# Products of the identity in TensorE's first idle time, and a scheduler that serves GpSimd before VectorE

## The chip, the cores and the metric

The kernel runs on one core of a Trainium2 chip, as one program and one launch. The metric is the device time of that launch in microseconds (us); smaller is better. The core has five engines with queues of their own: TensorE (PE; its weight loads are listed as PEld), VectorE (DVE), ScalarE (ACT), GpSimd (POOL) and SyncE (SP), which here only issues DMAs. Each engine takes its instructions strictly in the order of its own queue and waits at an instruction until what that one needs is there.

## The reference, cut to what matters

Three stages, all in float32. `x` is (8, 8, 512, 64): batch, heads, tokens, width; `state` is (8, 8, 32, 64).

```python
scores = scale * np.matmul(x, state.transpose(0, 1, 3, 2))     # softmax over the 32 states
xread  = np.matmul(softmax(scores), state)
scores2 = scale * np.matmul(state, x.transpose(0, 1, 3, 2))    # softmax over the 512 tokens
sread  = np.matmul(softmax(scores2), x)
x = concatenate([xread, sread], axis=2)     # to rows: 4608 x 512
x = (x @ w_a) * (x @ w_b) @ w_out           # first gated layer, 512 -> 1536 -> 512
g = x @ w_gate
out = silu(g) * (x @ w_val) @ w_out2        # second gated layer
```

The weights come as float64 words; the kernel makes float32 values of them on the chip. Products are made from two-part splits, three products for each (high by high, high by low, low by high).

## The kernel before

**Work and stages.** Tokens are worked on in blocks 0 to 7 of 512 columns and a block "s" with the 256 state rows. For the first layer the kernel multiplies states and weights first (`state_w`, tiles `sw`): each result goes to DRAM and comes back as `swr`, is split by ScalarE and VectorE into `swh` and `swl`, and TensorE then needs only the 32-wide softmax weights (`xs`) against it (`p`, line L624), followed by the output product `po` (L659). A name such as `p_1_2_0` is block 1, slice 2 of the inner 1536, side a. Blocks 0 to 3 take their first four slices in turn (list `TOGETHER`), so the early program is: scores `psc` (L505), softmax, `sw` products, `p` of blocks 0 and 1, and so on. The second layer (L729, L823) fills the second half of the program.

**Early chains.** A weight tile (`raw_w`, `raw_wo`) is loaded, converted by two ScalarE passes, a clamp (L384), a shift (L389) and a sign pass (L392) on VectorE and an integer add on GpSimd (L396). Then it is split: a ScalarE cast (L422 or L345) and a VectorE subtract (L338). `w_1` below is the second set of such tiles; `swl_0` is the low half that block 0 or 1 needs for slices 0 and 1, `swl_1` the one for slices 2 and 3.

**What sets the order.** `Program.order` is a list scheduler that runs while the program is built. Each piece of work is a Task with a planned duration for every engine that could do it, and a due time `by`. Time is advanced event by event; for each free engine the ready task with the earliest due time is taken, and the order of these picks becomes the order of the engines' queues. VectorE work with SBUF operands alone (`port`) and all GpSimd work exclude each other in the plan (`shared`, `blocked`). Engines are served in the order of the dict `ready`:

```python
ready = {e: [] for e in ("PE", "ACT", "DVE", "POOL", "DMA")}
```

Some subtracts, multiplies and clamps may go to VectorE or GpSimd (`dve_pool`). Short TensorE tasks are planned at double time as long as the main products have not begun (`main <= self.first`). The chip follows the queues alone; the planned times do not exist there.

Of the kernel before, what the change touches and what calls it, by code (L numbers as in the profile page):

```python
# [10 lines left out]
F32 = mybir.dt.float32  # L11
# [7 lines left out]
P = 128  # L19
# [41 lines left out]

ACT_US, DVE_US, FAST_US, POOL_US = ((0.09, 0.84e-3), (0.07, 1.05e-3), (0.07, 0.53e-3), (0.2, 2.6e-3))
# [3 lines left out]

BESIDE_US = 0.9
# [8 lines left out]
def dve(n, fast=False):  # L76
    a, b = FAST_US if fast else DVE_US
    return {"DVE": a + b * n}


def dve_pool(n):
    return dve(n) | {"POOL": POOL_US[0] + POOL_US[1] * n}
# [13 lines left out]
class Task:  # L96
    def __init__(self, i, engines, fn, bufs, deps, by, start, size):
        self.i, self.engines, self.fn, self.bufs, self.deps = i, engines, fn, bufs, deps
        self.by, self.start, self.size = by, start, size
        self.cost = min(engines.values())  # L100
        self.next = []
        self.new = []
        self.engine, self.main = None, 0.0

        self.port = False


class Program:
# [37 lines left out]
    def order(self):  # L146
# [4 lines left out]
        for t in reversed(tasks):  # L151
            for n in t.next:
                t.by = min(t.by, n.by - n.cost - HOP_US - (DMA_US + n.size / DMA_BYTES_PER_US if n.size else 0))
# [6 lines left out]
        main = 0.0  # L160
        ready = {e: [] for e in ("PE", "ACT", "DVE", "POOL", "DMA")}
# [12 lines left out]
        now, done = 0.0, []  # L174
        while events:
            now = events[0][0]
            main = max(main, min(now, self.first))
            while gates and gates[-1].start <= main:
                t = gates.pop()
# [4 lines left out]
            while events and events[0][0] <= now + 1e-9:  # L184
                _, kind, _, t = heapq.heappop(events)
# [8 lines left out]
            for e, heap in ready.items():  # L194
                if free[e] > now + 1e-9:
                    continue
                held = []
                blocked = shared > now + 1e-9 and e in ("DVE", "POOL")
                while heap:
                    item = heapq.heappop(heap)  # L200
                    t = item[2]
# [10 lines left out]
                    if e == "POOL" and "DVE" in t.engines and sum(  # L212
                        q[2].engines["DVE"] for q in ready["DVE"] if q[2].engine is None and not q[2].port
                    ) < BESIDE_US:
                        held.append(item)
                        continue
# [11 lines left out]
                    us = t.engines[e] * (2.0 if e == "PE" and t.engines[e] < 1.0 and main <= self.first else 1.0)  # L228
# [31 lines left out]
class Kernel:  # L260
# [80 lines left out]
    def hi_lo(self, src_buf, src, hi_buf, hi, lo_buf, lo, n, psum=False, **kw):  # L341

        hb = (hi_buf, 0) if hi_buf is lo_buf else hi_buf
        lb = (lo_buf, 1) if hi_buf is lo_buf else lo_buf
        self.p.add(act(n), lambda e: self.nc.scalar.copy(hi(), src()), [src_buf], [hb], **kw)  # L345
        self.subtract(
            lo, src, lambda: hi().bitcast(F32), dve(n) if psum else dve_pool(n), [src_buf, hb], [lb], **kw
        )
# [17 lines left out]
    def convert(self, src, name, start=0.0, by=1e9):  # L366

        nc = self.nc
# [13 lines left out]
        def clamp(e):  # L382
            f = t.t[:, 0].bitcast(F32)
            self.by_engine[e].tensor_scalar(  # L384
                out=f, in0=f, scalar1=SATURATED, scalar2=-SATURATED, op0=ALU.min, op1=ALU.max
            )

        self.p.add(dve(512, True) | {"POOL": 1.9}, clamp, [], [hi], **kw)
# [124 lines left out]
    def softmax1(self, b, g, sT, by):  # L513
# [11 lines left out]
        self.p.add(dve_pool(512), lambda e: self.by_engine[e].tensor_tensor(  # L525
# [14 lines left out]
        self.p.add(dve_pool(512), lambda e: self.by_engine[e].tensor_tensor(  # L540
# [6 lines left out]
    def softmax2(self, b, g, sT, by):  # L547
# [38 lines left out]
        self.pe(1.75, fn, [a2, xn], [ps], **kw)  # L586
# [277 lines left out]
    def body(self):  # L864
# [3 lines left out]
        p.add({"POOL": 1.2}, lambda e: make_identity(nc, self.ident.t), [], [self.ident], by=0.0)  # L868
        self.sread = Buf(None, "sread", lambda: self.sb.tile([P, NPAIR, ST], F32, name="sread"))
# [159 lines left out]
```

## Time and profile before

| | us |
|---|---|
| median of 3 runs (1513.57 to 1515.39) | 1514.61 |
| the profiled execution, its own time | 1514.56 |
| span of its trace | 1512.8 |
| TensorE busy in the span | 1471.7 (97%) |
| VectorE busy | 1069.6 (71%) |
| ScalarE busy | 649.5 (43%) |
| GpSimd busy | 111.9 (7%), 84 instructions |

The span runs from the first to the last instruction of the trace. Busy shares are means over stages that differ, so the rows further down are taken from stretches. In rows of the timeline the first two numbers are the start and the length in us, "x4" counts merged instructions, and the square bracket gives the idle time in front and what ended it. A float32 product that is not split shows as two MATMUL records.

### The profile page before, as it was taken

The numbers are of one execution on the slowest core, as the hardware profiler recorded it, in microseconds if no ns is written. First come the engines' busy times: TensorE is split into PE (matmuls) and PEld (weight loads), VectorE is DVE, ScalarE is ACT, GpSimd is POOL, SyncE is SP. The second block draws the span as 40 slices with busy tenths as digits, with TensorE's granted clock in tenths as the row PEclk, the third lists the DMA queues.
The fourth block names the chain that finished last, engine by engine and source line by source line (L and its number), as shares of the span: only waits on it lengthen the run. The fifth ranks groups of instructions, "written<-read, shape, count | busy, mean of one in ns | idle before, by whom it ended". The sixth has DMA issues, their size and how long they took to land.

```text
span 1512.8 us, 19096 instructions
## 1 busy us (share of the span) xinstructions
PE 1471.7 (97%) x6760; PEld 1213.7 (80%) x6760; DVE 1069.6 (71%) x1792; ACT 649.5 (43%) x1148; POOL 111.9 (7%) x84
## 2 busy tenths in 40 slices
PE   5699999999999999999999999999999999999998
PEld 2477788788888888998888888888888888888887
DVE  7989848865778787776777996556854677535554
ACT  6567756653556565654433441222322223222220
POOL 2212201200011111111000100000000000000000
PEclk7899999999999999999999999999999999999999
DMA  8575554652556565765965796455573456423412
GB/s 305 182 277 181 200 213 179 212 207 97 179 190 216 181 232 207 251 233 203 386 246 204 280 354 233 170 183 208 220 259 128 161 192 221 182 99 138 155 56 70
DMA packets 111183, 305.87 MB, mean 202 GB/s; under 512 B 11760, under 2 KB 12784, under 8 KB 111088
## 3 DMA queue, kind: packets, MB, share of 16 engines
q1 hardware_dynamic: 111088, 304.66, 56.1%
q8 instruction: 53, 0.87, 0.2%
q14 instruction: 42, 0.34, 0.1%
HBM read 223.35 MB, written 80.74 MB: 201 GB/s over the span
## 4 chain that ended last, share of the span: by engine, by line
PE 80%; DVE 1%; DMA 0%; issue 0%; ACT 0%; SPq 0%; DVEq 0%; ACTq 0%
PE pu L823 17%; PE po L659 12%; PE p L624 11%; PE pC L729 9%; PE pB L729 9%; PE pA L729 9%; PE pD L729 4%; PE p_s L624 2%; PE pvs L624 1%; PE po_s L659 1%; PE pgs L624 1%; PE pus L823 1%; PE psr L584 1%; PE psc L505 1%; DMA swr<-sw 0%; PE sw L452 0%
## 5 line engine op out<-in xcount | busy, mean ns | idle before, releaser
L659 PE MATMUL po<-hs,wo 128*128 128x512 f32 x1152 | 285.5, 392 | 0.0
L659 PEld LDWEIGHTS po<-hs,wo 128*128 128x128 f32 x1152 | 215.6, 188 | 45.2 <-issue 1.0
L624 PE MATMUL p<-xs,swh 128*128 128x512 f32 x768 | 240.2, 394 | 1.0 <-DVE xs L338 0.5
L624 PEld LDWEIGHTS p<-xs,swh 128*128 128x128 f32 x768 | 144.0, 189 | 32.0 <-DVE a L643 1.1
L624 PE MATMUL p<-xs,swl 128*128 128x512 f32 x384 | 150.7, 392 | 9.0 <-DVE swl L338 8.8
L729 PE MATMUL pB<-x,w 128*128 128x512 f32 x576 | 146.2, 389 | 0.0
L729 PE MATMUL pA<-x,wg 128*128 128x512 f32 x576 | 146.2, 389 | 0.0
L823 PE MATMUL pu<-wo,hv 128*128 128x512 f32 x576 | 140.6, 390 | 0.0
L823 PE MATMUL pu<-wo,hu 128*128 128x512 f32 x576 | 138.5, 390 | 0.0
L729 PEld LDWEIGHTS pB<-x,w 128*128 128x128 f32 x576 | 108.2, 188 | 22.4
L729 PEld LDWEIGHTS pA<-x,wg 128*128 128x128 f32 x576 | 108.2, 188 | 22.4
L823 PEld LDWEIGHTS pu<-wo,hu 128*128 128x128 f32 x576 | 107.9, 188 | 22.2
L823 PEld LDWEIGHTS pu<-wo,hv 128*128 128x128 f32 x576 | 107.9, 188 | 22.2
L743 DVE TENSOR_TENSOR t<-c,pB 128x512 f32<-128x512 f32 x96 | 65.9, 686 | 82.5 <-PE pB L729 81.4
L643 DVE TENSOR_TENSOR a<-a,p 128x512 f32<-128x512 f32 x96 | 65.8, 685 | 79.5 <-PE p L624 68.4
L747 ACT ACTIVATE av<-t 128x512 f32<-128x512 f32 x48 | 30.3, 632 | 175.9 <-DVE t L743 175.8
L330 ACT COPY a<-p 128x512 f32<-128x512 f32 x81 | 47.5, 586 | 105.4 <-PE p L624 100.0
L624 PEld LDWEIGHTS p<-xs,swl 128*128 128x128 f32 x384 | 72.6, 189 | 25.1 <-DVE swl L338 9.8
L345 ACT CAST hs<-a 128x512 fp32r<-128x512 f32 x96 | 59.6, 621 | 60.5 <-DVE a L643 52.5
L338 DVE TENSOR_TENSOR hs<-a,hs 128x512 fp32r<-128x512 f32 x96 | 69.5, 725 | 14.0 <-ACT hs L345 13.3
L841 DVE TENSOR_TENSOR part<-part,pu 128x512 f32<-128x512 f32 x64 | 43.9, 685 | 47.5 <-PE pu L823 47.3
L729 PE MATMUL pC<-x,wv 128*128 128x512 f32 x288 | 73.2, 390 | 0.0
(175 smaller groups left out, 2343.1 us busy)
## 6 DMA issues: line engine op xcount, KB each, us to landing
w<-w SPq DMA_DIRECT2D x120, 512.0 KB, 5.1
sw<-swo SPq DMA_DIRECT2D x96, 256.0 KB, 2.5
wg<-w2g SPq DMA_DIRECT2D x48, 512.0 KB, 4.7
wv<-w2v SPq DMA_DIRECT2D x48, 512.0 KB, 4.9
wo<-w2o SPq DMA_DIRECT2D x48, 512.0 KB, 5.6
swr<-sw SPq DMA_DIRECT2D x47, 512.0 KB, 4.9
raw_w<-in_wab SPq DMA_DIRECT2D x24, 512.0 KB, 7.7
xt<-in_xt SPq DMA_DIRECT2D x32, 256.0 KB, 5.3
```

The costliest lines, as they stand in the source:

```text
L330: self.nc.scalar.copy(out(), in_())
L338: lambda e: self.by_engine[e].tensor_tensor(out=out(), in0=in0(), in1=in1(), op=ALU.subtract), r, w, **kw
L345: self.p.add(act(n), lambda e: self.nc.scalar.copy(hi(), src()), [src_buf], [hb], **kw)
L505: pe.matmul(ps.t, lhsT=l, rhs=r, start=n == 0, stop=n == len(pairs) - 1)
L624: pe.matmul(ps.t[:, :n], lhsT=l, rhs=r, start=i == 0, stop=i == last)
L643: self.vec(n, lambda v, a=a, pb=pb: v.tensor_tensor(out=a.t[:, :n], in0=a.t[:, :n], in1=pb.t[:, :n], op=ALU.mult), [pb], [a])
L659: pe.matmul(ps.t[:, :n], lhsT=wo[f].t[:, hw, c], rhs=hs.t[:, hh, :n], start=st, stop=sp)
L729: pe.matmul(ps.t, lhsT=w.t[:, hw, c], rhs=x.t[:, hx], start=start and i == n == 0, stop=stop and i == 1 and n == 2, skip_group_check=True)
L743: self.vec(512, lambda e: e.tensor_tensor(out=out.t, in0=ta(), in1=tb(), op=op), [a, b], [out])
L747: p.add(act(n), lambda e: nc.scalar.activation(out=a.t[:, :n], in_=g.t[:, :n], func=AF.Sigmoid), [g], [a])
L823: pe.matmul(ps.t, lhsT=h.t[:, hh, c], rhs=wo[f].t[:, hw], start=f == steps[0] and i == 0, stop=f == steps[-1] and i == 2)
L841: self.vec(w, lambda v: v.tensor_tensor(out=to(), in0=part.t[:, j % 2, :w], in1=ps.t[:, :w], op=ALU.add), [ps, (part, j)], [ok], by=by)
```

## The change: what it does

It adds 44 tasks, each of two 128x128 products of the identity with itself into a PSUM tile `warm` that nothing reads. Their due time is the latest of all and they take no part in the due times of others (`spare`); TensorE gets one wherever the plan finds it free. The scheduler serves GpSimd ahead of VectorE. Tasks that VectorE or GpSimd could do now belong to VectorE alone, and the rule with `BESIDE_US` is gone. Short TensorE tasks are planned at double time only in the first 8 us. The planned cost of `psr` falls from 1.75 to 1.0.

```diff
+WARM, COLD_US = 44, 8.0
...
-BESIDE_US = 0.9
-
...
-def dve_pool(n):
-    return dve(n) | {"POOL": POOL_US[0] + POOL_US[1] * n}
...
             for n in t.next:
+                if t.spare:
+                    break
                 t.by = min(t.by, n.by - n.cost - HOP_US - (DMA_US + n.size / DMA_BYTES_PER_US if n.size else 0))
...
-        ready = {e: [] for e in ("PE", "ACT", "DVE", "POOL", "DMA")}
+        ready = {e: [] for e in ("PE", "ACT", "POOL", "DVE", "DMA")}
...
-                    if e == "POOL" and "DVE" in t.engines and sum(
-                        q[2].engines["DVE"] for q in ready["DVE"] if q[2].engine is None and not q[2].port
-                    ) < BESIDE_US:
-                        held.append(item)
-                        continue
...
-                    us = t.engines[e] * (2.0 if e == "PE" and t.engines[e] < 1.0 and main <= self.first else 1.0)
+                    us = t.engines[e] * (2.0 if e == "PE" and t.engines[e] < 1.0 and now < COLD_US else 1.0)
...
-            lo, src, lambda: hi().bitcast(F32), dve(n) if psum else dve_pool(n), [src_buf, hb], [lb], **kw
+            lo, src, lambda: hi().bitcast(F32), dve(n), [src_buf, hb], [lb], **kw
...
-        self.p.add(dve(512, True) | {"POOL": 1.9}, clamp, [], [hi], **kw)
+        self.p.add(dve(512, True), clamp, [], [hi], **kw)
...
-        self.pe(1.75, fn, [a2, xn], [ps], **kw)
+        self.pe(1.0, fn, [a2, xn], [ps], **kw)
...
+        warm = self.ring("po3", 1, "warm", self.ps)
+
+        def idle(pe):
+            for i in range(2):
+                pe.matmul(warm.t[:, :P], lhsT=self.ident.t, rhs=self.ident.t, start=True, stop=True)
+
+        for _ in range(WARM):
+            self.pe(0.44, idle, [self.ident], [warm], by=1e8).spare = True
```

The two multiplies and subtracts of the softmax (`dve_pool(512)`) become `dve(512)` likewise. Since the whole order comes out of one pass of the scheduler, it moves everywhere; three places matter below.

TensorE at the start of the program. `psc` are the scores of block 0 and then block 1, `sw_0_0` the first states-by-weights product, which needs `w_0_0`. Before:

```order
L505 MATMUL psc_0_84<-xt_0_0_72,strt_70 128x512
L505 MATMUL psc_0_84<-xt_0_1_74,strt_70 128x512
L505 MATMUL psc_1_97<-xt_1_0_78,strt_70 128x512
L505 MATMUL psc_1_97<-xt_1_1_80,strt_70 128x512
L505 MATMUL psc_0_142<-xt_0_0_109,strt_103 128x512
L505 MATMUL psc_0_142<-xt_0_1_115,strt_103 128x512
L452 MATMUL sw_0_0_181<-w_0_0_126,st_hi 128x512
L453 MATMUL sw_0_0_181<-w_0_0_126,st_lo 128x512
```

Now:

```order
L869 MATMUL warm<-ident 128x128 x8
L501 MATMUL psc_0_93<-xt_0_0_72,strt_70 128x512
L501 MATMUL psc_0_93<-xt_0_1_74,strt_70 128x512
L869 MATMUL warm<-ident 128x128 x2
L501 MATMUL psc_1_109<-xt_1_0_83,strt_70 128x512
L501 MATMUL psc_1_109<-xt_1_1_87,strt_70 128x512
L869 MATMUL warm<-ident 128x128 x22
L501 MATMUL psc_0_177<-xt_0_0_121,strt_114 128x512
L501 MATMUL psc_0_177<-xt_0_1_131,strt_114 128x512
L869 MATMUL warm<-ident 128x128 x24
L448 MATMUL sw_0_0_246<-w_0_0_147,st_hi 128x512
L449 MATMUL sw_0_0_246<-w_0_0_147,st_lo 128x512
```

All 88 products of the identity stand in the queue ahead of the first `p` (18 of them directly ahead of the fourth `psc`), and the needed products keep their order among themselves.

VectorE in the stretch ahead of the first `p`. `sn`, `mx` and `sm` are softmax tiles, `swo` copies of finished `sw` products, `w` the low half of weight tiles. Before:

```order
L338 TENSOR_TENSOR w_0_2_177<-cv_w_0_2_118,w_0_2_177 64x512 x2
L525 TENSOR_TENSOR sn_0_100<-sn_0_100,mx_0_105 128x512
L525 TENSOR_TENSOR sn_1_122<-sn_1_122,mx_1_157 128x512
L523 TENSOR_REDUCE mx_0_218<-sn_0_162 128x16
L532 TENSOR_REDUCE sm_0_224<-sn_0_100 128x16
L332 COPY swo_0_3_232<-sw_0_3_212 128x512
L532 TENSOR_REDUCE sm_1_240<-sn_1_122 128x16
L332 COPY swo_0_4_245<-sw_0_4_228 128x512
L338 TENSOR_TENSOR w_0_3_242<-cv_w_0_3_132,w_0_3_242 64x512 x2
```

Now:

```order
L334 TENSOR_TENSOR w_0_2_213<-cv_w_0_2_135,w_0_2_213 64x512 x2
L334 TENSOR_TENSOR w_0_3_230<-cv_w_0_3_153,w_0_3_230 64x512 x2
L521 TENSOR_TENSOR sn_0_112<-sn_0_112,mx_0_119 128x512
L521 TENSOR_TENSOR sn_1_137<-sn_1_137,mx_1_171 128x512
L519 TENSOR_REDUCE mx_0_310<-sn_0_203 128x16
L380 TENSOR_SCALAR cv_w_1_0_201<-cv_w_1_0_201 128x512
L528 TENSOR_REDUCE sm_0_325<-sn_0_112 128x16
L521 TENSOR_TENSOR sn_0_203<-sn_0_203,mx_0_310 128x512
```

The last tile of the first set, `w_0_3`, moved ahead of the softmax; the `swo` copies left VectorE for ScalarE, and the third subtract (`sn_0_203`) came to it from GpSimd.

ScalarE around the first products of block 1. `a_1_0` is the copy of `p_1_0_0`, the first product of block 1; `w_1_*` are the casts that the products `sw_1` wait for. Before:

```order
L345 CAST hs_0_1_427<-a_0_1_394 128x512
L330 COPY swo_0_7_436<-sw_0_7_429 128x512
L330 COPY a_1_0_473<-p_1_0_0_450 128x512
L422 CAST w_1_0_490<-cv_w_1_0_160 64x512 x2
L345 CAST hs_1_0_504<-a_1_0_473 128x512
L422 CAST w_1_1_509<-cv_w_1_1_171 64x512 x2
L375 ACTIVATE cv_wo_2_517<-raw_wo_2_475 128x512
L422 CAST w_1_2_521<-cv_w_1_2_184 64x512 x2
```

Now:

```order
L326 COPY swo_0_7_524<-sw_0_7_513 128x512
L341 CAST hs_0_1_532<-a_0_1_479 128x512
L418 CAST w_1_0_535<-cv_w_1_0_201 64x512 x2
L418 CAST w_1_1_541<-cv_w_1_1_222 64x512 x2
L418 CAST w_1_2_549<-cv_w_1_2_238 64x512 x2
L418 CAST w_1_3_555<-cv_w_1_3_250 64x512 x2
L326 COPY a_1_0_583<-p_1_0_0_563 128x512
L326 COPY swo_1_0_592<-sw_1_0_578 128x512
```

The eight casts of `w_1` moved from behind the copy of `p_1_0_0` to ahead of it.

## Rows read from the trace of the kernel before

**Rows 1.** The page: its head, and busy time by engine.

```profile
span 1512.8 us, 19096 instructions
PE 1471.7 (97%) x6760; PEld 1213.7 (80%) x6760; DVE 1069.6 (71%) x1792; ACT 649.5 (43%) x1148; POOL 111.9 (7%) x84
```

**Rows 2.** Windows: stretch, length, busy us by engine, granted clock, DMA share, GB/s.

```profile
0.00:50.00 50.00, 32.21 (x70) 15.28 (x70) 39.68 (x71) 34.51 (x57) 7.95 (x12) 0.80 0.75 279
50.00:92.00 42.00, 27.74 (x104) 19.87 (x104) 36.93 (x51) 22.83 (x40) 12.78 (x8) 0.88 0.63 217
92.00:150.00 58.00, 57.49 (x249) 45.47 (x248) 54.58 (x103) 41.37 (x79) 10.13 (x8) 1.00 0.60 219
150.00:250.00 100.00, 98.28 (x445) 79.52 (x445) 70.44 (x124) 64.63 (x121) 16.92 (x12) 1.00 0.56 200
```

**Rows 3.** Timeline of TensorE: start, length, instruction, idle time in front.

```profile
14.91 1.96 PE L505 MATMUL psc<-xt,strt 128*128 128x512 f32 x4 [2.18 <-DMA xt<-in_xt]
...
36.22 3.75 PE L505 MATMUL psc<-xt,strt 128*128 128x512 f32 x4 [2.20 <-DMA xt<-in_xt]
...
41.95 0.62 PE L624 MATMUL p<-xs,swh 128*128 128x512 f32 x2
...
51.10 0.63 PE L624 MATMUL p<-xs,swh 128*128 128x512 f32 x2
60.55 0.80 PE L624 MATMUL p<-xs,swl 128*128 128x512 f32 x1 [8.81 <-DVE swl L338]
...
91.95 0.62 PE L624 MATMUL p<-xs,swh 128*128 128x512 f32 x2
```

**Rows 4.** Timeline of VectorE, 16 to 92 us.

```profile
16.38 1.76 DVE L392 SCALAR_TENSOR_TENSOR cv_w<-raw_w,cv_w 128x512 uint32<-128x512 uint32 x1
...
40.44 1.22 DVE L338 TENSOR_TENSOR swl<-swr,swh 128x1024 fp32r<-128x1024 f32 x1 [0.18 <-issue]
...
44.57 0.75 DVE L384 TENSOR_SCALAR cv_w<-cv_w 128x512 f32<-128x512 f32 x2
...
49.81 1.28 DVE L332 COPY swo<-sw 128x512 f32<-128x512 f32 x2
...
52.27 4.62 DVE L392 SCALAR_TENSOR_TENSOR cv_w<-raw_w,cv_w 128x512 uint32<-128x512 uint32 x4
...
58.22 2.28 DVE L338 TENSOR_TENSOR swl<-swr,swh 128x1024 fp32r<-128x1024 f32 x1
...
64.90 0.69 DVE L643 TENSOR_TENSOR a<-a,p 128x512 f32<-128x512 f32 x1 [0.85 <-ACT w L422]
...
90.50 1.23 DVE L338 TENSOR_TENSOR swl<-swr,swh 128x1024 fp32r<-128x1024 f32 x1 [1.48 <-ACT swh L345]
```

**Rows 5.** Timeline of GpSimd: the identity's end, the four adds of the tile set w_1.

```profile
1.01 0.29 POOL masks.py:199 TENSOR_SCALAR_AFFINE_SELECT ident<-ident 128x128 f32<-128x128 f32 x1
...
53.04 6.37 POOL L396 TENSOR_TENSOR cv_w<-cv_w 128x512 int32<-128x512 int32 x4 [22.54 <-DVE cv_w L392]
```

**Rows 6.** Timeline of ScalarE: the copy of block 1's first product, and what follows.

```profile
62.70 0.58 ACT L330 COPY a<-p 128x512 f32<-128x512 f32 x1 [10.81 <-PE p L624]
63.18 1.25 ACT L422 CAST w<-cv_w 64x512 fp32r<-64x512 f32 x2
```

**Rows 7.** Pieces of the chain that ended last: start, length, what.

```profile
286.33 2.72 PE p L624 x12
...
631.96 2.88 PE p_s L624 x24
```

**Rows 8.** Windows, narrower: the granted clock is the third number from the end.

```profile
20.00:30.00 10.00, 5.52 (x10) 2.62 (x10) 9.78 (x16) 8.26 (x15) 2.83 (x3) 0.50 0.67 263
63.00:64.00 1.00, 1.00 (x4) 0.81 (x3) 1.00 (x3) 0.98 (x3) 0.00 (x0) 0.50 0.16 53
```

**Rows 9.** Groups by line and shape: busy us, mean ns, idle before.

```profile
L505 PE MATMUL psc<-xt,strt 128*128 128x512 f32 x32 | 21.1, 788 | 9.2 <-DMA xt<-in_xt 9.1
```

**Rows 10.** Instructions of the tile a on VectorE, 90 to 180 us: ns, first and last start.

```profile
L643 DVE TENSOR_TENSOR a<-a,p x12: 676/687/690, 94.9 to 173.0; 128x512 f32<-128x512 f32 x12
```

More of the change, by code (lines that the diff above doesn't have):

```diff
@@ L105, in __init__ @@
         self.port = False
+        self.spare = False
 class Program:
@@ L383, in clamp @@
             f = t.t[:, 0].bitcast(F32)
-            self.by_engine[e].tensor_scalar(
+            nc.vector.tensor_scalar(
                 out=f, in0=f, scalar1=SATURATED, scalar2=-SATURATED, op0=ALU.min, op1=ALU.max
             )
-        self.p.add(dve(512, True) | {"POOL": 1.9}, clamp, [], [hi], **kw)
+        self.p.add(dve(512, True), clamp, [], [hi], **kw)
         self.vec(512, lambda v: v.tensor_scalar(
@@ L524, in softmax1 @@
         )
-        self.p.add(dve_pool(512), lambda e: self.by_engine[e].tensor_tensor(
+        self.p.add(dve(512), lambda e: self.by_engine[e].tensor_tensor(
             out=grouped(sn.t), in0=grouped(sn.t), in1=mx.t.to_broadcast([P, 16, NS]), op=ALU.subtract
@@ L539, in softmax1 @@
         self.vec(250, rest, [], [sm], **kw)
-        self.p.add(dve_pool(512), lambda e: self.by_engine[e].tensor_tensor(
+        self.p.add(dve(512), lambda e: self.by_engine[e].tensor_tensor(
             out=grouped(sn.t), in0=grouped(sn.t), in1=sm.t.to_broadcast([P, 16, NS]), op=ALU.mult
```

## The prediction

> **What bounds the kernel now.** I read the page first, then windows, then the timelines of the engines over the first 100 us. TensorE is busy 1471.7 of 1512.8 us [rows 1], so 41.1 us are idle. The windows show where: 17.8 us before 50, 14.3 us between 50 and 92, then 0.5 us up to 150 and 1.7 us up to 250 [rows 2]. From 92 us on TensorE sets the time, so this change can win only before that, plus small change up to 250. A product at full clock costs 2.72/12 = 0.227 us [rows 7]; time lost shows also as half clock: the granted clock was 0.50, which is 1.2 GHz, from 20 to 30 us and again at 63 us [rows 8], and four records of `psc` took 3.75 us at that level against 1.96 at 2.4 GHz [rows 3].
>
> Before 92 us it is VectorE that everybody waits for. It is busy 39.7 of the first 50 us (it has nothing to do for the first 9) and 36.9 of the next 42 [rows 2]. Three marks on TensorE tell the story [rows 3]. The first `p` starts at 41.95, right behind VectorE's `swl` of slices 0 and 1 for block 0 (40.44 to 41.66, [rows 4]). The first `p` of block 1 begins at 51.10 with its high half and then sits 8.81 us, until 60.55, for the next `swl`; VectorE is meanwhile at four sign passes that take 4.62 us for four and at a `swl` of 2.28 us where the first took 1.22 [rows 4], since GpSimd does four adds of 1.6 us each beside them [rows 5]. `p_1_2_0` starts at 91.95, behind the `swl_1` that ended at 91.73 [rows 4]. From there TensorE does not stop.
>
> **The change part by part.** The order of the changed program is known; I count instructions up to each mark and price them with rows.
>
> *First `p`.* Up to the end of that first `swl` VectorE had 54 instructions and now has 51: three copies of `swo` (1.28/2 = 0.64 us each) and one clamp (0.75/2 = 0.38) are gone, one softmax subtract of the same 128x512 comes from GpSimd (0.64) [rows 4]. Net 1.6 us less: 41.95 becomes 40.3. The copies go to ScalarE (44 instructions become 47 up to its `swh`), busy 34.5 of 50 us [rows 2]; its slack hides them, and without it they would cost the same 1.9 us there. `w_0_3` ahead of the softmax brings the last `sw` of the first set, and with it the DMA round trip to `swr`, some us forward, so `swl` still waits for VectorE's turn alone.
>
> *The warm products.* 88 products are 176 records, because a float32 product shows as two (32 records for the 16 `psc` products, [rows 9]). A record of 512 columns took 1.96/4 = 0.49 us at full and 3.75/4 = 0.94 at half clock [rows 3]; a quarter of the columns gives 0.12 and 0.23. The weight load that goes with each record is no shorter than the shape allows: 24 records of 256 columns took 2.88 us, 0.12 each [rows 7]. So 21.1 us at full clock. TensorE's real work before 40.3 us is 16 records of `psc` (7.8 us) and 22 `sw` products (5.0), 12.8 us in all; from 1.3 us, when the identity is ready [rows 5], 39.0 us are there, 26.2 of them free. 21.1 fit, with 5 to spare. Cost on the path: 0, hidden by VectorE's 40 us. If that cover is gone, a needed product waits behind up to 24 warm ones in a row, 48 records or 5.8 us. Gain of the clock itself: `sw` and the fourth `psc` run at 0.23 and 0.49 instead of 0.45 and 0.94, but VectorE's queue is later than they are, so I count nothing (bounds 0 and the 1.8 us by which that `psc` shortens).
>
> *First `p` of block 1.* Up to its `swl` VectorE had 82 instructions, now 79: five `swo` copies go (3.2 us), the subtract and a clamp that GpSimd had come (1.0). Net 2.2 us: 60.55 becomes 58.4. The stall itself stays, with the four sign passes and four adds in the same place; GpSimd's first turn in the plan changes no row there. The clock falls again, since no warm product is left that late.
>
> The GPSIMD Engine Reference of the Trainium skill, section 8, Key points, says that GpSimd contends only with VectorE instructions in a two-port mode or with two SBUF inputs. The multiply `a_0_1`, which reads PSUM and now stands among the four sign passes, would by that rule run inside an add and cost nothing: 0.6 us more gain than the sum below. The trace of before agrees as far as it goes, a sign pass beside an add took 1.76 us at 16.38 [rows 4]; it has no such multiply beside one.
>
> *Slices 2 and 3 (`p_1_2_0`).* ScalarE used to sit 10.81 us at the copy of `p_1_0_0` with the casts of `w_1` behind it, though GpSimd had finished the first of those tiles at 54.6 us (53.04 and one add of 1.6); they ran from 63.18 [rows 5, 6]. Now the casts stand ahead and run during the stall, so the `sw_1` products can start once VectorE has passed `swl`. Up to `swl_1` VectorE had 121 instructions, now 109. Gone are 16: twelve of 128x512 (0.64 each, 7.7), two clamp or shift passes (0.75), two of 16 columns (between 0 and 0.64 each by the wider ones; I take 0.4 for both); new are three copies and one clamp (2.3). Net 6.5 us. Between 60 and 91.73 VectorE also idled 4.7 us in five waits, from 0.85 at 64.90 to 1.48 at 90.50 [rows 4], mostly for late `p` products; I let it keep 2.5 (it now copies `sw_1_5` and `sw_1_6` itself and waits for them) and save 2.2. So `swl_1` ends at 91.73 - 8.7 = 83.0 and `p_1_2_0` starts at 83.2. TensorE agrees: from 58.4 it has 88 products ahead of `p_1_2_0` (19.9 us), 1.9 us of half clock as before, and waits. Before, 31.4 us held 104 products (23.6), the same 1.9 and 5.9 of waits, for `w_1` and for the two PSUM banks that `sw` shares; I take 2.5 of them, the banks' part: 82.7. But it had done 16 products more by that mark before (138 of them from the first `p`, now 122): 3.6 us. So it stands at 86.8 where it stood at 91.95, 5.1 us ahead.
>
> *After that.* Between 92 and 150 VectorE is busy 54.6 of 58 us [rows 2]: the lead lasts only if VectorE keeps up. Up to `a_3_3`, the last multiply that stands at 173.0 [rows 10], it has 258 instructions against 260, about 2.8 us less by the same prices, and has saved 2.2 us of idling: 5.0 us earlier, so the lead just holds. The five tasks that GpSimd loses by then are in that count. The planned cost of `psr` and the removed rules act through the order alone; the 1.7 us of idle TensorE in 150 to 250 are what they can win or lose there, and I leave them. Beyond 250 us TensorE is full and GpSimd's last moved task falls under it.
>
> Sum: 1514.56 - 5.1 = 1509.4 us. The profiled execution (1514.56) stands 0.05 under the median, so no correction; 1.8 us lie outside its span.
>
> **The rivals.**
> *VectorE takes the lead back.* For: 94% busy from 92 to 150 [rows 2], and a saving of idle time that I only estimated. Against: 2.8 us of work really go. If only those and no idling are saved, and TensorE's 1.7 us grow by one, 1514.56 - 2.8 + 1 = 1512.8.
> *The warm products run at half clock, slower than before.* Place: TensorE's queue ahead of the first `p`. Then 176 x 0.23 = 40.5 us, `psc` 15.0 and `sw` 22 x 0.45 = 9.9: with the 1.3 at the front the first `p` starts at 66.7 instead of 40.3. VectorE stands at its multiply of that `p` and loses most of the 26 us; with some 6 of them won back from the later stall, 1509.4 + 20 = 1529. It decides from 26.2/176 = 0.15 us a record on. For it: short records on an engine that had idled, and half clock for as long as 20 to 40 us. Against: the clock was back up by the time of the main products at 41.95, after `psc` alone had filled TensorE since 36.22 [rows 3], and here there are no such holes.
> TensorE: Matmul & The Clock Gate of the Trainium skill, Part 4, says that products in transpose mode do not engage the full clock. These are plain products, so by its words the rule does not reach them; no row here shows plain 128-column products on a TensorE that was idle.
> *The stall at block 1 shrinks as well.* If the adds fall otherwise between the sign passes, up to the 3.1 us that four passes and one `swl` lost to them (4.62 - 4 x 0.64, and 2.28 - 1.22, [rows 4]) come on top: 1506.3. Against it: the passes and the adds stand in the same order as before, and only `a_0_1` is new among them.
>
> **How the numbers follow.** Forecast 0.58, lead taken back 0.20, half clock 0.10, smaller stall 0.12. The forecast's own range is 1506 to 1512: idle saved 0 to 4.7 instead of 2.2, up to 0.9 of the clock's 1.8. The range 1504 to 1514.5 takes in the third rival and the first and leaves out the half clock and some tails. A measurement of this kernel tells 0.2%, 3 us, from no change: faster means below 1511.6. Forecast gives 0.53 faster and 0.05 same, the smaller stall 0.12 faster, the lead taken back 0.02 faster, 0.15 same and 0.03 slower, half clock 0.10 slower: 0.67, 0.20, 0.13.
>
> **What would show it.** Right: granted clock 1.00 through 20 to 40 us, warm records near 0.12 us; the first `p` near 40.3, TensorE's wait for `swl` ending near 58.4, `w_1` casts before the copy of `p_1_0_0`, `p_1_2_0` near 83, and less than 3 us of idle TensorE from there to 250. Wrong: the first `p` later than 42; a wait between 55 and 83 that the order did not have; idle TensorE of over 5 us between 83 and 180 with VectorE full.

## The result, and the profile after

The changed kernel takes 1501.75 us (median of 5 runs, 1501.54 to 1502.41), the kernel before 1514.61 us: a ratio of 0.9915 with a 95% interval of 0.9902 to 0.9929, 12.9 us faster. The forecast was 1509.4 us with 1504.0 as its lower end: the sign was right, and the gain is two and a half times the one forecast.

The page answers to [rows 1], its head first:

```profile
span 1499.8 us, 19474 instructions
...
PE 1480.6 (99%) x6936; PEld 1233.0 (82%) x6936; DVE 1058.6 (71%) x1792; ACT 650.3 (43%) x1154; POOL 102.8 (7%) x78
```

The windows answer to [rows 2]: stretch, length, busy us of TensorE, its weight loads, VectorE, ScalarE and GpSimd, granted clock, DMA share, GB/s.

```profile
0.00:50.00 50.00, 44.56 (x250) 35.09 (x250) 40.24 (x74) 37.06 (x62) 6.64 (x11) 1.00 0.80 297
50.00:92.00 42.00, 34.47 (x134) 26.24 (x135) 40.70 (x57) 24.95 (x42) 11.70 (x8) 0.88 0.80 295
92.00:150.00 58.00, 57.55 (x254) 46.16 (x252) 54.27 (x109) 43.89 (x83) 8.56 (x7) 1.00 0.48 162
150.00:250.00 100.00, 99.84 (x454) 81.55 (x455) 69.96 (x127) 66.35 (x125) 14.27 (x10) 1.00 0.57 205
```

The first row holds 250 records instead of 70 at a clock of 1.00 instead of 0.80: these are the warm products. The others hold the surprise. From 50 to 92 TensorE gets 134 records done instead of 104. From 92 to 250, where the prediction left things as they were, it is idle 0.6 us instead of 2.2. The stretch behind that, which the prediction called full, shows the same, before and then after: 2.3 us idle become 1.1.

```profile
250.00:400.00 150.00, 147.69 (x646) 120.32 (x645) 106.80 (x165) 78.34 (x131) 14.14 (x9) 1.00 0.51 176
```
```profile
250.00:400.00 150.00, 148.93 (x658) 122.14 (x657) 105.78 (x168) 78.37 (x131) 12.85 (x9) 1.00 0.51 177
```

TensorE's timeline, for [rows 3] (start, length, instruction, idle time in front and what ended it):

```profile
1.36 3.78 PE L869 MATMUL warm<-ident 128*128 128x128 f32 x16 [1.36 <-POOL ident masks.py:199]
...
10.18 5.07 PE L869 MATMUL warm<-ident 128*128 128x128 f32 x44
...
34.27 1.93 PE L501 MATMUL psc<-xt,strt 128*128 128x512 f32 x4
...
38.58 0.62 PE L620 MATMUL p<-xs,swh 128*128 128x512 f32 x2
...
48.13 0.63 PE L620 MATMUL p<-xs,swh 128*128 128x512 f32 x2
56.94 0.80 PE L620 MATMUL p<-xs,swl 128*128 128x512 f32 x1 [8.18 <-DVE swl L334]
...
58.82 0.63 PE L448 MATMUL sw<-w,st_hi 128*128 128x512 f32 x1
...
79.53 0.61 PE L620 MATMUL p<-xs,swh 128*128 128x512 f32 x2
```

The warm products start at 0.24 us a record (3.78/16) and run at 0.115 (5.07/44) from then on. The first 16 run at half the later pace, but the windows list a granted clock of 1.00 there too, so no row names them half clock. The `psc` that took 3.75 us now takes 1.93. The first `p` starts at 38.58. The first `p` tile of block 1 (48.13) gets its `swl` at 56.94, and directly behind that tile stands a product of `w_1` (58.82), which before came at 71.53. VectorE, for [rows 4]:

```profile
37.25 1.22 DVE L334 TENSOR_TENSOR swl<-swr,swh 128x1024 fp32r<-128x1024 f32 x1
...
48.66 1.28 DVE L388 SCALAR_TENSOR_TENSOR cv_w<-raw_w,cv_w 128x512 uint32<-128x512 uint32 x2
49.86 0.68 DVE L639 TENSOR_TENSOR a<-a,p 128x512 f32<-128x512 f32 x1
50.46 2.83 DVE L388 SCALAR_TENSOR_TENSOR cv_w<-raw_w,cv_w 128x512 uint32<-128x512 uint32 x2
...
54.61 2.28 DVE L334 TENSOR_TENSOR swl<-swr,swh 128x1024 fp32r<-128x1024 f32 x1
...
57.52 6.68 DVE L334 TENSOR_TENSOR w<-cv_w,w 64x512 fp32r<-64x512 f32 x8
...
77.54 1.22 DVE L334 TENSOR_TENSOR swl<-swr,swh 128x1024 fp32r<-128x1024 f32 x1
```

GpSimd's four adds, for [rows 5], and ScalarE's casts of `w_1` ahead of the copy of `p_1_0_0`, for [rows 6]:

```profile
49.49 6.32 POOL L392 TENSOR_TENSOR cv_w<-cv_w 128x512 int32<-128x512 int32 x4 [29.61 <-DVE cv_w L388]
```
```profile
51.10 1.25 ACT L418 CAST w<-cv_w 64x512 fp32r<-64x512 f32 x2
52.77 1.26 ACT L418 CAST w<-cv_w 64x512 fp32r<-64x512 f32 x2 [0.41 <-POOL cv_w L392]
54.44 2.66 ACT L418 CAST w<-cv_w 64x512 fp32r<-64x512 f32 x4 [0.41 <-POOL cv_w L392]
59.10 0.59 ACT L326 COPY a<-p 128x512 f32<-128x512 f32 x1 [2.00 <-issue]
```

The whole chain of `w_1` is through at 64.2 us, where VectorE's last subtract ends; before, it was 76.5 (70.79 + 5.71). How far a kernel stands ahead is read at two marks below: the start of the first `psr` and of the first `p_s`, taken from the instructions of that tile on TensorE. Before, then after:

```profile
L584 PE MATMUL psr<-xn,a x128: 377/379/380, 139.4 to 610.1; 128*128 128x256 f32 x128
```
```profile
L624 PE MATMUL p_s<-xss,w1s x288: 277/283/284, 616.2 to 669.1; 128*128 128x256 f32 x144
```

```profile
L580 PE MATMUL psr<-xn,a x128: 377/379/382, 130.6 to 597.1; 128*128 128x256 f32 x128
```
```profile
L620 PE MATMUL p_s<-xss,w1s x288: 277/283/283, 603.3 to 656.1; 128*128 128x256 f32 x144
```

So the lead is 8.8 us at 131 us, and 12.9 at 603; from there to the end nothing is added.

### The profile page after: what moved, and what is told of

Its sections match the earlier page's. It is cut to its first block, busy times and chain, and to the rows that moved or that the text cites. A ratio compares the mean times of both kernels' runs of the same rounds, so it can differ in the third digit from the quotient of the medians.

```text
span 1499.8 us, 19474 instructions
## 1 busy us (share of the span) xinstructions
PE 1480.6 (99%) x6936; PEld 1233.0 (82%) x6936; DVE 1058.6 (71%) x1792; ACT 650.3 (43%) x1154; POOL 102.8 (7%) x78
## 4 chain that ended last, share of the span: by engine, by line
PE 82%; DVE 1%; issue 0%; ACT 0%; DVEq 0%; ACTq 0%
PE pu L819 17%; PE po L655 12%; PE p L620 12%; PE pC L725 9%; PE pB L725 9%; PE pA L725 9%; PE pD L725 4%; PE p_s L620 2%; PE pvs L620 1%; PE po_s L655 1%; PE pgs L620 1%; PE pus L819 1%; PE psr L580 1%; PE psc L501 1%; DVE w L334 0%; PE sw L448 0%
```

## The experiments

All against the kernel before on the same chip, four to eleven runs each. The marks are those of the one traced run, and say where a difference arises.

| run | what it is | median us | ratio to before (95%) | first psr | first p_s |
|---|---|---|---|---|---|
| | before | 1514.61 | | 139.4 | 616.2 |
| | after | 1501.75 | 0.9915 (0.9902 to 0.9929) | 130.6 | 603.3 |
| e1 | after, products not issued | 1504.28 | 0.9930 (0.9918 to 0.9943) | 132.0 | 605.3 |
| e2 | after, psr at its old cost | 1501.96 | 0.9916 (0.9902 to 0.9929) | 131.6 | 604.4 |
| e3 | after, VectorE first | 1511.80 | 0.9988 (0.9978 to 0.9998) | 137.0 | 612.9 |
| e10 | after, choice of engine back | 1505.75 | 0.9941 (0.9929 to 0.9954) | 134.1 | 608.0 |
| e14 | after, old half-speed rule | 1502.54 | 0.9920 (0.9907 to 0.9934) | 130.8 | 603.8 |
| e7 | before, GpSimd first | 1504.95 | 0.9937 (0.9925 to 0.9950) | 131.5 | 605.9 |
| e8 | before, warm products | 1513.09 | 0.9993 (0.9984 to 1.0002) | 135.7 | 613.6 |
| e5 | after, VectorE first to 65 us | 1509.46 | 0.9962 (0.9949 to 0.9976) | 139.1 | 611.1 |
| e6 | after, VectorE first from 65 us | 1508.50 | 0.9962 (0.9949 to 0.9974) | 132.6 | 609.1 |
| e9 | before, w_1 forward, sT behind it | 1516.52 | 1.0011 (1.0002 to 1.0020) | 141.7 | 618.4 |
| e13 | before, w_1's casts forward | 1513.39 | 0.9991 (0.9983 to 1.0000) | 137.6 | 615.5 |
| e12 | after, w_1's casts back | 1504.87 | 0.9936 (0.9923 to 0.9948) | 133.5 | 606.4 |
| e4 | after, 70 warm tasks | 1502.13 | 0.9915 (0.9902 to 0.9929) | 129.6 | 603.1 |
| e11 | e7 with its gaps filled | 1505.91 | 0.9938 (0.9925 to 0.9952) | 134.2 | 608.8 |

### One part of the change undone

**e1.** The planner does all that it does in the changed kernel, so every engine has the same order; only the warm products themselves are not issued.

```diff
-            for i in range(2):
+            for i in range(0):
                 pe.matmul(warm.t[:, :P], ...
```

> The changed kernel's order on every engine, but the 44 warm tasks issue no product (they still take their place in the plan). If the clock that the warm products hold is worth something, the time rises by it: the needed products ahead of the first p run at half clock again (psc 3.75 instead of 1.9 us, sw 0.45 instead of 0.23), the first p goes from 38.6 back towards 41 us, and the time is 1503.5 to 1505. If the order alone made the gain, as the prediction counted, VectorE is the later one and the time stays within 0.5 us of 1501.75.

1504.28 us, 2.5 over the changed kernel. Its first window, and its first `p`:

```profile
0.00:50.00 50.00, 31.36 (x74) 15.57 (x74) 39.32 (x72) 37.07 (x62) 6.10 (x10) 0.80 0.79 292
```
```profile
40.23 0.62 PE L620 MATMUL p<-xs,swh 128*128 128x512 f32 x2
```

The clock is back at 0.80, and the first `p` at 40.23. That is within 0.1 us of the 40.3 that the prediction counted out of VectorE's order, but VectorE does not set it. TensorE's fourth `psc`, then VectorE's `swl`:

```profile
34.34 3.75 PE L501 MATMUL psc<-xt,strt 128*128 128x512 f32 x4 [3.77 <-DMA xt<-in_xt]
```
```profile
37.40 1.22 DVE L334 TENSOR_TENSOR swl<-swr,swh 128x1024 fp32r<-128x1024 f32 x1
```

The `swl` is done at 38.62, 1.6 us ahead of the `p`. TensorE comes to the `p` straight from the slow `psc` and six `sw` products, without a wait in front. With the clock kept up the same row ends 1.65 us earlier, at 38.58. At the end the products are worth 2.5 us by the medians (2.0 between the two traced runs), and since the order is the same, the clock is what they bring.

**e2.** The planned cost of `psr` back at its old value.

```diff
-        self.pe(1.0, fn, [a2, xn], [ps], **kw)
+        self.pe(1.75, fn, [a2, xn], [ps], **kw)
```

> The changed kernel with the planned cost of psr back at 1.75. The order is the same on TensorE up to instruction 367 and on VectorE up to 208, so the trace up to some 125 us must not change. If the 4.2 us that the changed kernel wins between 139 and 320 us come from this number, the time is near 1506. If they come from VectorE's lighter load and the lead it brings, the time stays at 1501 to 1503.

1501.96 us: no difference, as the second expectation said. The number does not bring what was won behind 139 us.

**e3.** VectorE served ahead of GpSimd again, all else as changed.

```diff
-        ready = {e: [] for e in ("PE", "ACT", "POOL", "DVE", "DMA")}
+        ready = {e: [] for e in ("PE", "ACT", "DVE", "POOL", "DMA")}
```

> The changed kernel with VectorE served ahead of GpSimd again, as in the kernel before. If GpSimd's first turn matters, the four adds of the first weight set come later, w_0 moves back behind the softmax on VectorE, and the first p comes later by 1 to 3 us: 1503 to 1505. If only the removed choice of engine and the warm tasks in the plan matter: 1501.5 to 1502.5.

1511.80 us, far outside both expectations: ten of the 12.9 us are gone. The eleven runs lie wide, six from 1509.8 to 1511.8 and five from 1514.0 to 1516.1, so the ten are rather too few than too many; the traced run is the median. GpSimd (in a row, then the shortest, median and longest of the four adds in ns), then VectorE, then TensorE:

```profile
51.86 9.67 POOL L392 TENSOR_TENSOR cv_w<-cv_w 128x512 int32<-128x512 int32 x4 [31.54 <-DVE cv_w L388]
```
```profile
L392 POOL TENSOR_TENSOR cv_w<-cv_w x4: 1452/1726/4873, 51.9 to 59.8; 128x512 int32<-128x512 int32 x4
```
```profile
51.03 2.49 DVE L388 SCALAR_TENSOR_TENSOR cv_w<-raw_w,cv_w 128x512 uint32<-128x512 uint32 x4
...
70.95 4.27 DVE L334 TENSOR_TENSOR w<-cv_w,w 64x512 fp32r<-64x512 f32 x6
```
```profile
55.05 0.80 PE L620 MATMUL p<-xs,swl 128*128 128x512 f32 x1 [5.19 <-DVE swl L334]
...
71.70 0.79 PE L448 MATMUL sw<-w,st_hi 128*128 128x512 f32 x1 [2.98 <-DVE w L334]
72.29 0.63 PE L449 MATMUL sw<-w,st_lo 128*128 128x512 f32 x1
```
```profile
159.59 0.52 PE L448 MATMUL sw<-w,st_hi 128*128 128x512 f32 x1 [2.12 <-DVE swo L328]
```

The `swl` of the stall comes 1.9 us earlier than in the changed kernel (55.05 against 56.94), so this is not a longer stall. What is late is `w_1`: the sign passes start at 51.03 instead of 48.66, the first of the four adds takes 4.87 us, from 51.86 on, where it took some 1.6 in the changed kernel (6.32/4; the other three are near that here too), the last subtract ends at 75.2 instead of 64.2, and TensorE waits 2.98 us for it and then runs at 0.63 a product for 6 us. Far from there, at 157.5, it waits another 2.12 us, for a copy of `sw`.

**e10.** The tasks that VectorE or GpSimd may take, and the rule that holds GpSimd back from them, put back (the diff of the change shows all the lines).

```diff
-            lo, src, lambda: hi().bitcast(F32), dve(n), [src_buf, hb], [lb], **kw
+            lo, src, lambda: hi().bitcast(F32), dve(n) if psum else dve_pool(n), [src_buf, hb], [lb], **kw
```

> The changed kernel with the tasks for VectorE or GpSimd and the rule that holds GpSimd back from them put back; warm products, GpSimd first, the half-speed rule and psr stay. Theory 1 (the removal is worth little, as GpSimd first alone gave nearly all beside the clock): 1501.5 to 1504. Rival (with GpSimd first, tasks that it may take from VectorE hold the shared port and cost what the removal gave): 1505 to 1510.

1505.75 us, 4.0 over the changed kernel: the rival's range, not the theory's. GpSimd:

```profile
42.24 2.13 POOL L344 TENSOR_TENSOR xs<-at,xs 128x512 fp32r<-128x512 f32 x1 [19.69 <-ACT xs L351]
...
52.31 9.53 POOL L402 TENSOR_TENSOR cv_w<-cv_w 128x512 int32<-128x512 int32 x4 [7.36 <-DVE cv_w L398]
```

GpSimd takes a subtract of `xs` and a clamp, and has its adds of `w_1` 2.8 us later than the changed kernel (52.31 against 49.49), at 9.53 us for four, of which the first takes 4.93, as in e3. It was not too busy to begin them: it sat 7.36 us for VectorE's sign passes, which come at 51.54 here and at 48.66 there. So the removal of the choice acts through VectorE's order as well; why the planner puts the sign passes later was not tried.

**e14.** The old rule for half-speed products.

```diff
-(2.0 if e == "PE" and t.engines[e] < 1.0 and now < COLD_US else 1.0)
+(2.0 if e == "PE" and t.engines[e] < 1.0 and main <= self.first else 1.0)
```

> The changed kernel with the old rule for half-speed products (twice the time for short products until the first gate, instead of up to 8 us). Theory 1 (the rule moves few instructions, and is worth nothing of its own): 1501.5 to 1503. Rival (the planner then holds TensorE for slower than it is while the warm products keep its clock up, and puts the first products late): 1504 to 1508.

1502.54 us, 0.8 over the changed kernel; the two intervals overlap for the most part, so this is not told from nothing, as the first expectation said.

### One part alone on the kernel before

**e7.** The line of e3, the other way round, on the kernel before.

```diff
-        ready = {e: [] for e in ("PE", "ACT", "DVE", "POOL", "DMA")}
+        ready = {e: [] for e in ("PE", "ACT", "POOL", "DVE", "DMA")}
```

> The kernel before with one line changed: GpSimd is served ahead of VectorE. No warm products, the old rule for the half-speed products, VectorE-or-GpSimd tasks and their rule as before, psr at 1.75. Theory 1 (the turn alone brings the w_1 weights forward, and is worth its some 10 us without the rest): 1504 to 1506.5, the w_1 casts of ScalarE ahead of the copy of a_1_0. Rival (the turn works only behind the warm start, whose order feeds the stall; alone it moves little): 1511 to 1515.

1504.95 us: two names that change places give 9.7 of the 12.9 us, without a warm product. TensorE's wait for `swl` is gone altogether, and the row that shows why is GpSimd's:

```profile
46.13 2.40 POOL L338 TENSOR_TENSOR swl<-swr,swh 128x1024 fp32r<-128x1024 f32 x1 [12.86 <-ACT swh L345]
54.01 6.29 POOL L396 TENSOR_TENSOR cv_w<-cv_w 128x512 int32<-128x512 int32 x4 [5.48 <-DVE cv_w L392]
```

Served first, GpSimd takes that `swl` from VectorE and has it done at 48.5 (60.5 before). Its adds of `w_1` come 1 us later than before (54.01 against 53.04). ScalarE casts `w_1` from 55.72 on (63.18 before), behind the copy of `a_1_0` at 53.53 and not ahead of it. So the time lies in the first theory's range, but the sign that it named is missing. This is not the mechanism of the changed kernel, where only VectorE may make `swl`.

**e8.** The warm tasks and their `spare` mark alone.

```diff
+        for _ in range(WARM):
+            self.pe(0.44, idle, [self.ident], [warm], by=1e8).spare = True
```

> The kernel before with the warm products alone: VectorE served first, the old rule for half-speed products, tasks for either engine as before. Theory 1 (the products are worth the clock, 2.5 us, and no order): 1511.5 to 1513, granted clock 1.00 from 20 to 40 us, the stall at swl as long as before, near 10 us. Rival (they also move the order by what they take in the scheduler, and most of the gain comes with them): 1503 to 1508.

1513.09 us, an interval that touches 1, and just above the first theory's range. The first `psr` is 3.7 us earlier, but `p_s` only 2.6: behind it TensorE waits in 150 to 250 us, as in e3 and with the same 2 us:

```profile
161.59 0.50 PE L456 MATMUL sw<-w,st_hi 128*128 128x512 f32 x1 [2.06 <-DVE swo L336]
```

### Where GpSimd's turn counts

**e5, e6.** GpSimd first only from 65 us of the planner's clock on (e5), or only up to there (e6).

```diff
-            for e, heap in ready.items():
+            for e in ("PE", "ACT", "POOL", "DVE", "DMA") if now > 65.0 else ("PE", "ACT", "DVE", "POOL", "DMA"):
+                heap = ready[e]
```

In e6 the condition is `now < 65.0`.

> The changed kernel with one edit: up to 65 us of the scheduler's own clock VectorE is served ahead of GpSimd, as before the change; from then on GpSimd is. With VectorE first throughout, the time was 1511.8 us. Theory 1 (the turn matters at the start-up stall alone, where GpSimd's four adds decide when the weights of w_1 are ready): 1511 to 1512, the first w_1 subtracts again in two pieces that end after 70 us, the first psr near 137. Theory 2 (the turn matters in the blocks that follow, where it keeps VectorE free of GpSimd's adds): 1502 to 1504, whatever the order at the stall.

> The mirror of the run above: GpSimd first up to 65 us of the scheduler's clock, VectorE first from then on. Theory 1 (the stall decides): 1501.5 to 1503, all eight w_1 subtracts in one piece that ends near 64 us, psr near 131. Theory 2 (the later blocks decide): 1509 to 1512, psr near 131 but the p_s block near 612.

Neither theory came true. VectorE first at the stall alone costs 7.7 us (e5), from 65 us on alone 6.8 (e6), both together 10.0 (e3): by the medians the two halves do not add. Why is open: at the first `psr` e3 has lost 6.4 us and e5, with the same plan up to 65 us, 8.5. In e5 one add of `w_1` takes 4.89 us, as in e3. In e5 the loss is all there at the first `psr` and TensorE then does not wait at all from 150 to 250. In e6 it is 2.0 us at `psr` and 5.8 at `p_s`, with the wait of e3 and e8 again:

```profile
156.19 0.53 PE L449 MATMUL sw<-w,st_hi 128*128 128x512 f32 x1 [2.45 <-ACT swo L327]
```

Most of the rest of the loss in e6 is in that stretch too: TensorE is idle 3.0 us from 150 to 250 (0.2 in the changed kernel), and its clock falls, 150 to 180 us have 0.94.

### Is it the place of the w_1 chain?

**e9.** On the kernel before, behind the planner: ScalarE's eight casts of `w_1` ahead of the copy of `a_1_0`, VectorE's eight subtracts behind its add of `a_1_0`.

```diff
+        put([t for c, w in ks for t in of("POOL", c)[-1:] + of("ACT", c, w)], copy)
+        put([add] + [t for c, w in ks for t in of("DVE", c, w)],
+            next(t for t in done[done.index(add) + 1:] if t.engine == "DVE"))
```

> The kernel before with its planner unchanged; after the planner, w_1's four products for ScalarE (eight casts) are moved ahead of the copy of a_1_0 behind which they stood 10.8 us, and VectorE's eight subtracts of w_1 directly behind its add of a_1_0 (before they stood behind the copies of a_1_1 and sT). TensorE's order is as before. Theory 1 (what GpSimd's turn gives at the stall is that w_1 is ready sooner): the waits for w behind the first psc (2.25, 0.31 us) go, 2 to 4 us of the time with them: 1510.5 to 1513. Rival (the order of w_1 is worth nothing while TensorE's own order stays): 1514 to 1516.

1516.52 us, slower, and outside both expectations. TensorE:

```profile
73.03 0.50 PE L465 MATMUL sw<-w,st_hi 128*128 128x512 f32 x1 [3.56 <-DVE sT L345]
...
75.20 0.80 PE L465 MATMUL sw<-w,st_hi 128*128 128x512 f32 x1 [1.44 <-ACT swo L343]
```

The waits for `w` (2.25, 0.31) are gone, and a longer one stands there, for the copy `sT`, which now comes behind the eight subtracts: TensorE's next bank is free only when it is done. The clock fell as well, from 70 to 92 it was 0.84 where it had been 1.00. The run shows how a wait is passed on, not what `w_1` is worth.

**e13.** The same with the casts forward and the first two subtracts only, so that `sT` keeps its place.

```diff
+        i = q.index(of("ACT", "p0_1_0_0", "a0_1_0")[0])
+        q[i:i] = casts
+        q, first = lines["DVE"], [t for c, w in ks[:1] for t in of("DVE", c, w)]
...
+        i = q.index(of("DVE", "p0_1_0_1", "a0_1_0")[0]) + 1
+        q[i:i] = first
```

> The kernel before with ScalarE's eight casts of w_1 ahead of its copy of a_1_0 and VectorE's first two subtracts of w_1 alone behind its add of a_1_0; the copies of a_1_1 and sT keep their place ahead of the other six, so that TensorE's bank is not held as in the run where all eight subtracts stood ahead of sT. Theory 1 (readiness of w_1 costs what its waits show, and TensorE's next bank comes free at 70.0 us): the wait of 2.25 us falls to under 1, the waits of 0.62 and 0.31 behind it go, and the time is 1511.5 to 1513.5. Rival (the next late step takes the place of the wait): 1514 to 1516.

1513.39 us: a gain of 1.4 us whose interval ends at 1.0000. The wait of 2.25 us became 0.32; the mark `psr` is 1.8 us earlier, `p_s` 0.7. In the theory's range, at its weak end.

**e12.** On the changed kernel, ScalarE's casts of `w_1` behind the copy of `a_1_0` again; every other engine's order is untouched.

```diff
+        for t in casts:
+            q.remove(t)
+        i = q.index(of("ACT", "p0_1_0_0", "a0_1_0")[0]) + 1
+        q[i:i] = casts
```

> The changed kernel with one engine's order touched: ScalarE's eight casts of w_1 stand behind its copy of a_1_0 again, as in the kernel before, where they stood ahead of it. Every other engine's order, the warm products and the planner stay. Theory 1 (what GpSimd's turn gives at the stall is that the w_1 chain, adds then casts then subtracts, is through by 64 us): the casts run from about 59.7 to 65, the subtracts from about 61 on, TensorE's first product of w_1 at 58.8 waits 2 to 3 us, and the time is 1503.5 to 1507. Rival (the chain's place is worth nothing by itself): 1501.5 to 1502.5.

1504.87 us, 3.1 over the changed kernel. ScalarE, then TensorE:

```profile
58.97 0.59 ACT L344 COPY a<-p 128x512 f32<-128x512 f32 x1 [7.91 <-PE p L638]
59.45 5.12 ACT L436 CAST w<-cv_w 64x512 fp32r<-64x512 f32 x8
```
```profile
56.81 0.80 PE L638 MATMUL p<-xs,swl 128*128 128x512 f32 x1 [8.20 <-DVE swl L352]
...
60.84 0.79 PE L466 MATMUL sw<-w,st_hi 128*128 128x512 f32 x1 [1.95 <-DVE w L352]
```

The copy sits 7.91 us, eight casts behind it, and TensorE's first product of `w_1` waits 1.95 us; the clock from 60 to 70 is 0.78 instead of 0.96. `psr` is 2.9 us later and `p_s` 3.1: the whole price arises here and is carried to the end. So in the changed kernel the place of eight casts on one engine is worth 3.1 us. It is no share of the ten of e3: there the first add is not done before 56.7, and the casts could not have begun at 51.

### Attempts at a faster kernel

**e4.** More warm tasks, of which 42 products stand ahead of `p_1_0_0`.

```diff
-WARM, COLD_US = 44, 8.0
+WARM, COLD_US = 70, 8.0
```

> The changed kernel with 70 warm tasks instead of 44; the order on the other engines is the same but for 4 instructions, and 21 of the new tasks stand ahead of p_1_0_0, where TensorE waits 8.2 us for swl. If half clock after that wait costs what the rows say (six products and two sw at 0.43 instead of 0.23, about 1.9 us), the granted clock stays at 1.00 and the time falls to some 1500. If the warm products outlast the wait (84 records at 0.11 are 9.5 us against 9.0), up to 0.7 us of that is lost. If VectorE alone sets the time up to 80 us, nothing changes: 1501.75.

1502.13 us, the same as the changed kernel. The clock is 1.00 throughout and no wait for `swl` shows: 84 records stand in the stall and run to 57.5, where the changed kernel goes on at 56.94. `psr` is 1.0 us earlier, `p_s` 0.2. TensorE waits again between 150 and 250:

```profile
150.00:250.00 100.00, 99.23 (x452) 80.87 (x451) 69.56 (x126) 65.50 (x123) 13.25 (x10) 1.00 0.58 202
```

**e11.** The order of e7 on every engine, and warm products put behind the planner into the gaps that its clock shows on TensorE.

```diff
+        for t in pe:
+            n = int((min(t.at, WARM_END_US) - last - 0.3) / 0.5)
+            if n > 0 and idle:
+                i = done.index(t)
+                done[i:i], idle = idle[:n], idle[n:]
+            last = max(last, t.end)
```

> The kernel before with GpSimd served first (1504.95 us alone), in exactly that order on every engine, and warm products set into the gaps that the planner's own clock shows on TensorE up to 80 us, 36 pairs of them, so that they move no other instruction. Theory 1 (the two parts add: the order from GpSimd's turn, and 2.5 us of clock from the products): 1501.5 to 1503, granted clock 1.00 from 20 to 40 us, and no half-speed stretch behind the wait for w near 61 to 67 us. Rival (the products stand in the way where the planner's gaps are not the chip's): 1504 to 1507.

1505.91 us, no faster than e7 without them, as the rival said:

```profile
50.88 3.29 PE L888 MATMUL warm<-ident 128*128 128x128 f32 x28
53.92 0.71 PE L639 MATMUL p<-xs,swh 128*128 128x512 f32 x2
```

At 50.9 us the planner sees a gap in which 14 products fit; the chip has a shorter one. The 28 records hold `p_1_0_0` to 53.92, which began at 49.61 in e7, the `psc` behind that block starts at 59.48 instead of 57.42, and `psr` comes 2.7 us later (the traced run is the slowest of five). In the changed kernel the planner places the products itself and reckons with what they take. No run beats the changed kernel.

## Why the prediction was wrong

The sum said a lead of 5.1 us; it is 12.9. By its own steps:

*First `p`, 40.3.* The step "so I count nothing" for the clock failed. It rested on VectorE's queue being the later one, and at this mark it is not. By the count `swl` would end at 40.1 (41.66 less 1.6); it ended at 38.62 in e1 and at 38.47 after, since VectorE also began 0.5 us earlier (8.39 instead of 8.86) and lost a wait of 0.77 us at 12.8. TensorE's own row, at half clock, then set the first `p`: 40.23 in e1, 38.58 at full clock. So 40.23 beside the 40.3 is luck. The bound of 1.8 us was named; the real value is 1.65 at this mark, and 2.5 in the time. At the next mark, 56.94 against 58.4, the lead is 1.5 us greater than said.

*Warm products.* Right: 0.115 us a record where 0.12 was said, 0.24 for the first 16 where 0.23 was said of half clock, no cost on the path, and the clock falls again in the stall. The half-clock rival fell with that: behind the first 16 records the products run at 0.115 us with a granted clock of 1.00, which is 2.4 GHz.

*The stall.* Right as a row: 8.18 us against 8.81, the adds 6.32 against 6.37, the `swl` 2.28 us again. The multiply `a_0_1`, beside an add, took its usual 0.68 us at 49.86. That agrees with the GPSIMD Engine Reference of the Trainium skill, section 8, Key points, which names VectorE instructions in a 2-port mode or with two SBUF inputs as the ones that contend; the multiply has one of its inputs in PSUM. The two sign passes behind it took 1.41 us each on the mean (2.83/2). The prediction was wrong that the trace of before has no multiply beside an add: one at 122.40 took 0.68 us beside adds that run from 121.36. The third rival, that passes and adds lie better, came true with 0.5 us of its 3.1 (1.28 + 2.83 against 4.62).

*Slices 2 and 3.* The mechanism was right: casts of `w_1` at 51 instead of 63, ahead of the copy, products of `w_1` early. The size was off. `p_1_2_0` starts at 79.53 with 16 products fewer done, which puts it 8.8 us ahead and not 5.1. Of the 3.7, 1.5 come with the start; most of the rest is TensorE's waits between 57 and 79.5, of which the sum kept 2.5 us and which are 0.28 and 0.31. VectorE did not "keep 2.5" of its idling either: behind `w_1` it had 0.51 and 0.38.

*"So the lead just holds"*, and *"Beyond 250 us TensorE is full"*. This is the term that failed most: it put the gain behind 92 us at nothing, and the lead grows from 8.8 to 12.9 us between 131 and 603. TensorE was not full: before, it sat idle 2.3 us between 250 and 400. In windows, TensorE's idle time from 92 to 400 us was 0.51 + 1.72 + 2.31 and is 0.45 + 0.16 + 1.07, which is 2.9 us of the 4.1. In these rows the product behind a wait is also longer (0.50 against 0.39 us); the rest of the remaining 1.2 I cannot assign to rows. The sum left out the 1.7 us of idle in 150 to 250, though the new order acts in the whole program. That GpSimd's turn from 65 us on is worth 6.8 us in the changed kernel is shown (e6). Three runs with VectorE first there (e3, e6, e8) have a wait of 2.1 to 2.5 us ending between 156 and 162, and no run with GpSimd first has one above 0.85 from 150 to 250. But the kernel before, e9 and e13 serve VectorE first as well and have none above 0.74, so the turn alone does not make that wait. The number for `psr` has no part in it (e2).

*What GpSimd's turn is worth.* The prediction held that it "changes no row" at the stall, and gave it no term. The stall is as it was, but undone in the changed kernel the turn costs 10.0 us (e3), and alone on the kernel before it gives 9.7 (e7). The two numbers are alike and the rows are not: in e7 GpSimd makes the `swl` of the stall, in e3 `w_1` is late. Shown for the changed kernel: the turn from 65 us on is worth 6.8 us (e6), and the place of the `w_1` casts 3.1 (e12). Not shown is how the loss at the stall in e3 divides between sign passes that start 2.4 us later, one add that takes 3.3 us longer, and the casts behind it. Undone one by one the parts add to 2.5 + 10.0 + 4.0 + 0.8 + 0.2 = 17.5 us, more than the 12.9. Part of that may be the one long add, which stands in e3, e5 and e10 (4.87, 4.89, 4.93 us) and in no other run; it was not tried apart. Which instruction of VectorE or GpSimd makes the wait between 156 and 162 stays open.

## What to carry to other kernels

Where a planner writes the order, a change of which engine is asked first can outweigh the part with the most lines; ask which long chain hangs on that engine and which tasks it can now take from another, and follow both to the end, not only to the stall that the profile shows. Two runs with nearly the same number, such as e3 and e7, can have different causes; read the rows of each. An early order is worth something only if nothing else that the waiting engine needs moves behind it (e9), and each part is best priced by undoing it in the final kernel and by doing it alone in the first. Filling idle time to keep a clock up paid here where the filled engine itself was the later one (e1), and brought nothing where the filler outlasted the wait (e4) or the gap was only in the plan (e11).

## What was not expected of the hardware

GpSimd and VectorE slow one another, and which of them gives way differs from run to run. In the kernel before, after and in e7 the four adds take 6.3 to 6.4 us, and VectorE is slowed: in the changed kernel the later two sign passes take 1.41 us on the mean, and the `swl` 2.28. In e3 VectorE keeps its pace, 0.62 us a sign pass (2.49/4) and 1.22 for the `swl`, and GpSimd's first add takes 4.87 us where a single add in the changed kernel took 1.30 (at 74.91); e5 and e10 show the same. Who started first does not decide it: in the kernel before, too, the sign passes were going (52.27) when the first add began (53.04). What does is not shown, and spans on GpSimd are rough. With plain products of 128 columns in TensorE's idle time the granted clock stayed at 1.00 through the first 50 us, at 0.115 us a record; without them it was 0.80 (e1).
